# VectorE order in the gate/up stage of a fused attention and MLP kernel: filler sums moved behind quadrant 0, early fill begun three quads sooner

## The chip, the core and the metric

The kernel runs on one core of a Trainium2 chip. The metric is the time of one execution in microseconds of the device ("us"). A profile is one execution recorded by the hardware; its span runs from the core's first instruction to its last and was 1.7 to 1.8 us shorter than the time of the same execution. TensorE is PE, VectorE is DVE, ScalarE is ACT, and SP issues the DMA transfers used here. L851 is line 851 of the kernel.

## The reference, cut to what matters

```python
x = A_x                                    # [1, 2048, 1024] bf16
h = x + attention(layernorm(x), A_wqkv, A_wo)      # linear attention, 32 heads
y = layernorm(h)
gate = y @ W_gate                          # [1024, 3584]
up   = y @ W_up
hh   = where(gate > 0, gate, 0) * up       # Relu(gate) * up
h2   = h + hh @ W_down                     # [3584, 1024]
```

The stage in question is gate, up and their product (gate/up), some 287 to 584 us of the trace; the down projection follows.

## The kernel before

The kernel multiplies by a scheme with seven block products instead of eight (m1 to m7, each 8 matmuls: four contraction steps for gate and four for up). In gate/up a **quad** is the four output quadrants of one block of features. Every group of four quads shares a second-level product of 28 matmuls, p1 to p7, spread over the first quad of the group: that first quad's time is called the product window here. TensorE accumulates in three kinds of PSUM bank, ACT copies snapshots out, and DVE adds a snapshot to a bank (`gu`), after which ACT applies the Relu and DVE multiplies:

```python
# in quad()
def m(n, nm, t=None):                       # 8 matmuls into bank A, D or E
    ...
            nc.tensor.matmul(ps[:, v, :], lhsT=w[v][n - 1][:, kc, :], rhs=left[n - 1][:, kc, :], ...)   # L851
def snap(nm):
    nc.scalar.copy(out=st[nm][:], in_=halves(st["A"]))                                            # L856
def gu(q, nm, base):
    g = st[q] = mwork.tile([P, 2, SW], BF16, tag="gu", name="gu")
    add(out=g[:], in0=halves(st[nm]), in1=st[base][:], op=ALU.add)                                # L860
    nc.scalar.activation(out=g[:, 0, :], in_=g[:, 0, :], func=ACT.Relu)                           # L861
def mul(q):
    add(out=out[q], in0=st[q][:, 0, :], in1=st[q][:, 1, :], op=ALU.mult)                          # L864
def mul2():
    add(out=out[2], in0=halves(st["A"])[:, 1, :], in1=st["rg"][:], op=ALU.mult)                   # L871
    hh_sums_a(hq, s, fc)                                                                          # L700-702
# [... cut ...]
"g0": lambda: gu(0, "A", "r") if first is not None else gu(0, "D", "m1"),
"m6": lambda: m(6, "A"), "m3": lambda: m(3, "E"), "m4": lambda: m(4, "A"), "g3": lambda: gu(3, "E", "u3"),
"g1": lambda: gu(1, "E", "u2"), "x1": lambda: (mul(1), hh_sums_b(hq, s, fc)),   # hh_sums_b: L708
# [... cut ...]
```

Two pairs matter: m6 accumulates into bank A once g0 has read it, and m3 accumulates into bank E (accX or accY by turns) once g3 has read it. Between these reads DVE does small sums that later quads and the down projection need, here called filler. They are the sums of the next quad's weights (L642 to 648), of the second-level operands (L893 to 896, L919), of four rows of hh that an earlier stage spilled to HBM, and of W_down:

```python
def wd_sums(c):
    ...
    def one():
        t = fpool.tile([P, FQ * SW], BF16, tag="wt", name="wt")       # a single buffer
        ...
        tt(out=st["t"][0], in0=b12, in1=b11, op=ALU.subtract)         # L680
    def two(): ...                                                    # L683
    def three(): ...                                                  # L686
    def four():
        tt(...)                                                       # L689
        for k in range(4):
            nc.sync.dma_start(out=t_dram[k][:, 2 * c:2 * c + 2, :], in_=st["t"][k])   # L691
    return load, [one, two, three, four]

def hh_sums_a(hq, s, f):
    ...
    nc.vector.tensor_tensor(out=s1, in0=hq[:, H21, :], in1=hq[:, H22, :], op=ALU.add)   # L700
    nc.vector.tensor_tensor(out=s2, in0=s1, in1=h11, op=ALU.subtract)                   # L701
    nc.vector.tensor_tensor(out=s3, in0=h11, in1=hq[:, H21, :], op=ALU.subtract)        # L702
    nc.sync.dma_start(out=x_dram[s][k][:, H22:S3 + 1, r, :], in_=hq[:, H22:S3 + 1, :])

def early_sums(f):                          # one spilled row: 5 pieces, two of them empty
    ...
    return [load, lambda: None, lambda: None, lambda: hh_sums_a(st[0], 0, f), lambda: hh_sums_b(st[0], 0, f)]
```

The filler of one quad lies in a list `work`, which six slots empty in program order. PE, DVE and ACT run in that order; only the order of DMA issue is left to a scheduler. There are 24 quads: four alone, then five groups of four.

```python
def slot(n):
    for _ in range(-(-len(work) // (SLOTS - n))):       # SLOTS = 6
        work.pop(0)()
# per quad, k counts quads, r counts feature blocks
if grouped:
    want = -(-len(fill) // max(nwin - 2 - k, 1))        # nwin = 24; fill: 55 pieces
    for p in range(want):
        work.insert(min(len(work), 2 * p + 1), fill.pop(0))
elif r in (1, 2):
    for p in range(2 if r == 1 else 1):
        work.append(cross_sums.pop(0))
# product window (first quad of a group); x is the second-level product, prv the quad before
x["p1"](); x["c1"](); prv["g3"](); x["p2"](); x["j00"](); prv["m4"]()
slot(0)
prv["x3"](); prv["m3"](); prv["rg"](); prv["x2"](); x["p6"](); x["c2"](); x["p5"](); prv["g1"]()
slot(1)
prv["x1"](); cur = quad(s, f, w, res[s, fi]); cur["m1"](); x["p7"](); x["c3"]()
slot(2)
cur["g0"](); cur["m5"]()
# [... cut: next weights' loads ...]
x["j11"](); slot(3); cur["m6"](); cur["s2"](); cur["x0"](); x["p4"](); x["c4"]()
slot(4); x["p3"](); x["j01"](); cur["m7"](); cur["s3"](); slot(5)
# [... cut: the other quads ...]
if k == nwin - 3:
    for x in range(2):
        ...
        load_w(0, x)                                    # first W_down tiles, 896 KB each, L977
```

(Statements are joined on lines here to save room.)

## Time and profile before

The median is 738.5 us over 3 runs, 736.57 to 738.87; the profiled run has a span of 734.7 us. By stretch, from the table of windows (busy us of each engine):

| stretch, us | length | PE busy | DVE busy | ACT busy |
|---|---|---|---|---|
| 0 to 287.2 (attention, first MLP rows) | 287.2 | 278.96 | 214.07 | 192.03 |
| 287.2 to 584 (gate/up) | 296.8 | 293.71 | 250.31 | 128.91 |
| 584 to 734 (down projection) | 150.0 | 146.90 | 116.05 | 4.05 |

TensorE is busy nearly throughout, and DVE for 84% of gate/up. A busy share does not tell a lost half microsecond, however, since records of matmuls overlap, and a few are missing. Gaps in this document are therefore taken from starts: 0.2157 us is laid against every matmul, and what the next start has beyond that is a gap (lost records show as whole multiples of 0.2157 behind a group of less than four, and are left out). Before the change gate/up has five, one in each group; the prediction shows their lines. Gaps here are good to about 0.01 us: their sum is 2.56 us in the prediction and 2.55 in the tables.

### The profile page before, as it was taken

Reading aid. Unit: us, or ns where it says so; the run is one execution under the profiler, and the core shown is the slowest. Engines: PE = TensorE matmul, PEld = TensorE weight load, DVE = VectorE, ACT = ScalarE, POOL = GpSimd, SP = SyncE. Lnnn points to the kernel's source line nnn. Section 1 sums busy time; section 2 is a strip of 40 time slices with the busy share of each in tenths; the row PEclk is TensorE's granted clock in tenths of the full one; section 3 lists DMA queues with packets and bytes.
Section 4 is the critical chain, followed back from the end, with each engine's and each line's share of the span. In section 5 each row is a group of like instructions: output and inputs, shape, how many; then the busy total and the mean of one; then the engine's idle time right before and its main releaser. Section 6 shows DMA issues by size and latency. Waiting matters only on the chain.

```text
span 734.7 us, 10578 instructions
## 1 busy us (share of the span) xinstructions
PE 719.6 (98%) x3947; PEld 380.0 (52%) x4000; DVE 580.4 (79%) x1039; ACT 325.0 (44%) x580; POOL 20.8 (3%) x56
## 2 busy tenths in 40 slices
PE   8999999999999999999999999999999999999997
PEld 3444555444444444444444444444444468888567
DVE  6998644677789767789897898989987379996677
ACT  4876553778886655444444444444444220000000
POOL 1000000000000000000000000000000001100210
PEclk9999999999999999999999999999999999999999
DMA  9765002079986524167348558685574499977932
GB/s 316 168 147 158 0 1 93 24 163 228 232 166 159 136 73 137 43 172 212 98 135 258 180 183 249 210 239 197 187 243 134 144 392 337 311 258 276 258 44 58
DMA packets 144708, 128.89 MB, mean 175 GB/s; under 512 B 50960, under 2 KB 127888, under 8 KB 144656
## 3 DMA queue, kind: packets, MB, share of 16 engines
q1 hardware_dynamic: 137584, 123.30, 55.5%
q0 software_dynamic: 5312, 3.15, 3.6%
q10 hardware_dynamic: 1760, 1.77, 0.7%
q8 instruction: 31, 0.51, 0.3%
q14 instruction: 21, 0.17, 0.1%
HBM read 76.81 MB, written 39.85 MB: 159 GB/s over the span
## 4 chain that ended last, share of the span: by engine, by line
PE 67%; DVE 18%; ACT 7%; DMA 5%; issue 2%; SPq 0%; DVEq 0%; ACTq 0%; POOL 0%
PE accA L851 15%; PE accA L1345 8%; PE attn L557 5%; PE accX L851 4%; PE Aq L314 3%; DVE gu L860 3%; PE accA L1171 3%; PE accY L851 3%; PE Aq L738 3%; PE accX L1345 3%; PE Aq L454 3%; PE accY L1345 2%; PE Eq L314 2%; PE accY L1171 2%; PE accX L1171 2%
## 5 line engine op out<-in xcount | busy, mean ns | idle before, releaser
L861 ACT ACTIVATE gu<-gu 128x512 bf16<-128x512 bf16 x72 | 45.5, 632 | 84.0 <-DVE gu L860 84.0
L856 ACT COPY snap<-accA 128x1024 f32<-128x1024 f32 x52 | 52.5, 1012 | 65.2 <-PE accA L851 65.0
L851 PEld LDWEIGHTS <-tg 128*128 128x128 f16 x384 | 37.5, 98 | 47.9 <-issue 3.2
L851 PEld LDWEIGHTS <-tu 128*128 128x128 f16 x384 | 37.6, 98 | 45.3
L557 PE MATMUL attn<-wo_mem,oT 128*128 128x512 bf16 x247 | 57.9, 379 | 1.9 <-DVE o_sb L534 1.2
L851 PE MATMUL accA<-hn,tg 128*128 128x512 f16 (+1 forms) x192 | 49.3, 379 | 0.0
L851 PE MATMUL accA<-hn,tu 128*128 128x512 f16 (+1 forms) x192 | 49.3, 379 | 0.0
L154 ACT COPY u<-Aq 128x512 f32<-128x512 f32 x54 | 31.4, 583 | 36.4 <-PE Aq L314 19.1
L1345 PEld LDWEIGHTS <-x 128*128 128x128 f16 (+1 forms) x448 | 43.8, 98 | 5.5
L557 PEld LDWEIGHTS <-oT 128*128 128x128 bf16 x256 | 24.6, 98 | 31.8 <-issue 3.4
L860 DVE TENSOR_TENSOR gu<-accX,snap 128x1024 bf16<-128x1024 f32 x26 | 31.7, 1221 | 10.6 <-ACT snap L856 8.3
L860 DVE TENSOR_TENSOR gu<-accY,snap 128x1024 bf16<-128x1024 f32 x26 | 31.7, 1220 | 7.5 <-ACT snap L856 7.5
L851 PEld LDWEIGHTS <-wu 128*128 128x128 bf16 x208 | 20.4, 98 | 24.5
L851 PEld LDWEIGHTS <-wg 128*128 128x128 bf16 x208 | 20.4, 98 | 24.5
L314 PEld LDWEIGHTS <-xT 128*128 128x128 bf16 (+1 forms) x192 | 18.6, 98 | 23.5 <-issue 2.1
L534 DVE TENSOR_TENSOR o_sb<-nd,rd 128x384 bf16<-128x384 f32 (+1 forms) x48 | 23.4, 509 | 8.3 <-ACT rd L533 6.1
L1309 POOL DMA_DIRECT2D out_dram<-o x12 | 15.2, 1265 | 506.5 <-DVE o L1305 504.7
L1345 PEld LDWEIGHTS <-xs 128*128 128x128 f16 x280 | 27.4, 98 | 3.2
L560 DVE SCALAR_TENSOR_TENSOR x_res<-attn,x_res 128x512 bf16<-128x512 f32 x32 | 22.0, 687 | 8.5 <-PE attn L557 8.4
L1351 DVE TENSOR_TENSOR snap<-accA,u 128x1024 f32<-128x1024 f32 x16 | 19.5, 1221 | 11.4 <-PE accA L1345 11.3
L864 DVE TENSOR_TENSOR hq<-gu 128x512 bf16<-128x512 bf16 x48 | 20.3, 423 | 10.3 <-ACT gu L861 10.3
L1171 PEld LDWEIGHTS <-x 128*128 128x128 bf16 (+1 forms) x168 | 16.5, 98 | 19.6
(268 smaller groups left out, 1508.9 us busy)
## 6 DMA issues: line engine op xcount, KB each, us to landing
x<-x_dram SPq DMA_DIRECT2D x17, 896.0 KB, 8.5
x_dram<-hq SPq DMA_DIRECT2D x28, 512.0 KB, 3.1
wg<-in_B_W_gate_dram SPq DMA_DIRECT2D x14, 512.0 KB, 4.9
wu<-in_B_W_up_dram SPq DMA_DIRECT2D x14, 512.0 KB, 6.6
x_dram<-hq SPq DMA_DIRECT2D x28, 256.0 KB, 2.4
wraw<-in_B_W_down_dram SPq DMA_DIRECT2D x14, 512.0 KB, 5.1
t_dram<-wt SPq DMA_DIRECT2D x21, 256.0 KB, 2.4
xd<-x_dram SPq DMA_DIRECT2D x6, 896.0 KB, 6.7
```

The lines of the kernel that those rows point to most:

```text
L154: copies[nm, v] = nc.scalar.copy(out=snaps[nm, v], in_=bank[v][:])
L314: nc.tensor.matmul(ps[:], lhsT=left[m - 1][:, kc, r + v * P:r + (v + 1) * P], rhs=right[m - 1][:, kc, :], start=(start and kc == 0), stop= ...
L454: nc.tensor.matmul(ps[:], lhsT=rq[m - 1][:, kc, (c + v) * P:(c + v + 1) * P], rhs=left[m - 1][:, kc, :], start=(start and kc == 0), stop=( ...
L534: nc.vector.tensor_tensor(out=ov[:, c0:c0 + n], in0=ndv[:, :, 0:P].rearrange("p k (h e) -> p k h e", h=HPC), in1=rd[:, 0:n, :].unsqueeze(3 ...
L557: nc.tensor.matmul(ps[:], lhsT=st["oT"][:, c, :], rhs=wo_sb[:, c, j * NW:(j + 1) * NW], start=(c == 0), stop=(c == KC - 1))
L738: nc.tensor.matmul(ps[:], lhsT=w(v, m)[:, kc, :], rhs=left[m - 1][:, kc, :], start=(start and kc == 0), stop=(kc == KH - 1), skip_group_ch ...
L851: nc.tensor.matmul(ps[:, v, :], lhsT=w[v][n - 1][:, kc, :], rhs=left[n - 1][:, kc, :], start=(t is not None and kc == 0), stop=(kc == KH - ...
L856: nc.scalar.copy(out=st[nm][:], in_=halves(st["A"]))
L860: add(out=g[:], in0=halves(st[nm]), in1=st[base][:], op=ALU.add)
L861: nc.scalar.activation(out=g[:, 0, :], in_=g[:, 0, :], func=ACT.Relu)
L1171: nc.tensor.matmul(ps[:, t * NW:(t + 1) * NW], lhsT=x_tile(n, s, kh)[:, f, (t0 + t) * P:(t0 + t + 1) * P], rhs=w_tile(n, kh)[:, f, :], sta ...
L1345: nc.tensor.matmul(pv[:, tt, :], lhsT=left(m)[:, f, tt * P:(tt + 1) * P], rhs=right(m)[:, f, :], start=(t is not None and f == 0 and tt % ...
```

## The change

Intent: take the filler away from the place ahead of g0, where it holds up m6, and put it next to the second-level join behind it; let the first two slots of the product window take less; and begin the fill at the second quad rather than the fifth, so that fewer pieces fall into each later window.

```diff
-    def slot(n):
-        for _ in range(-(-len(work) // (SLOTS - n))):
+    def slot(n, parts=0):
+        for _ in range(-(-len(work) // (parts or SLOTS - n))):
             work.pop(0)()
...
-            if grouped:
+            if r in (1, 2):
+                for p in range(2 if r == 1 else 1):
+                    work.append(cross_sums.pop(0))
+            if k:
                 want = -(-len(fill) // max(nwin - 2 - k, 1))
                 for p in range(want):
                     work.insert(min(len(work), 2 * p + 1), fill.pop(0))
-            elif r in (1, 2):
-                for p in range(2 if r == 1 else 1):
-                    work.append(cross_sums.pop(0))
...
                 prv["m4"]()
-                slot(0)
+                slot(0, 9)
                 prv["x3"]()
...
                 prv["g1"]()
-                slot(1)
+                slot(1, 8)
                 prv["x1"]()
...
                 x["c3"]()
-                slot(2)
                 cur["g0"]()
+                slot(2, 4)
                 cur["m5"]()
```

## The prediction

> **What bounds the kernel now.** I read the page's busy times, the chain, the table of windows over gate/up (287 to 584 us), the waits of that stretch, then the timeline wherever a matmul starts late.
>
> ```profile
> PE 719.6 (98%) x3947; PEld 380.0 (52%) x4000; DVE 580.4 (79%) x1039; ACT 325.0 (44%) x580; POOL 20.8 (3%) x56
> ...
> PE 67%; DVE 18%; ACT 7%; DMA 5%; issue 2%; SPq 0%; DVEq 0%; ACTq 0%; POOL 0%
> ```
> TensorE is the bound; DVE's 18% of the chain suggests more than there is, since much of it ran beside matmuls.
>
> ```profile
> 344.00:392.00 48.00, 47.43 (x216) 21.52 (x220) 42.37 (x86) 21.61 (x28) 0.00 (x0) 1.00 0.49 158
> ```
> Columns: window, length, then busy us and count of PE, weight loads, DVE, ACT. One group of four quads is four times six steps of 8 matmuls plus one second-level product of 28, so 220. Eight matmuls take 1.73 us in the chain, 0.2157 each: 220 make 47.45 us. Groups follow each other every 47.8 us, so a group loses about 0.4 us, although DVE is 88% busy.
>
> ```profile
> PE accA L851 <- DVE gu L860: 1.8, 4, 0.8
> ```
> This is the only wait of TensorE in the whole stretch.
>
> I then laid 0.2157 us per matmul against all starts. Where 0.21 us is missing a group shows x3 for x4: a lost record. Five real gaps remain, each at m6, which accumulates into bank A, behind quadrant 0's `gu<-accA`:
>
> ```profile
> 344.31 1.02 PE L851 MATMUL accA<-hs,tg 128*128 128x512 f16 x4 [0.83 <-DVE gu L860]
> 392.12 1.02 PE L851 MATMUL accA<-hs,tg 128*128 128x512 f16 x4 [0.17 <-DVE gu L860]
> 439.98 1.02 PE L851 MATMUL accA<-hs,tg 128*128 128x512 f16 x4 [0.22 <-DVE gu L860]
> 487.60 1.02 PE L851 MATMUL accA<-hs,tg 128*128 128x512 f16 x4
> 535.80 1.02 PE L851 MATMUL accA<-hs,tg 128*128 128x512 f16 x4 [0.56 <-DVE gu L860]
> ```
> By start-to-start they are 0.99, 0.33, 0.38, 0.14 and 0.72 us: 2.56 us, or 0.35% of 738.5. That is all this change can win in gate/up.
>
> DVE ahead of the first gap:
>
> ```profile
> 340.77 0.43 DVE L864 TENSOR_TENSOR hq<-gu 128x512 bf16<-128x512 bf16 x1 [0.43 <-ACT gu L861]
> 341.23 0.42 DVE L708 TENSOR_TENSOR hq<-hq 128x512 f16<-128x512 bf16 x1
> 341.57 0.42 DVE L647 TENSOR_TENSOR tu<-wu 128x512 f16<-128x512 bf16 x1
> 341.91 0.42 DVE L700 TENSOR_TENSOR hq<-hq 128x512 f16<-128x512 bf16 x1
> 342.36 0.43 DVE L701 TENSOR_TENSOR hq<-hq,x 128x512 f16<-128x512 f16 x1
> 342.70 0.42 DVE L702 TENSOR_TENSOR hq<-x,hq 128x512 f16<-128x512 bf16 x1
> 343.04 1.22 DVE L860 TENSOR_TENSOR gu<-accA,snap 128x1024 bf16<-128x1024 f32 x1
> ```
> Here 647 and the spilled-row sums 700 to 702 are filler; g0 (L860) ran from 343.04 to 344.26 because of them, and m6 would have started at 343.32.
>
> **What the Trainium skill says.** "TensorE: Matmul & The Clock Gate", section "Wait — 56ns, not 53.3ns?": warm 512-column matmuls start 215.7 ns apart; the trace agrees (1.73 us for 8; each record shows 379 ns). "VectorE: DVE Perf Modes", "The perf-mode tier table": tensor_tensor runs 2x on bf16 in SBUF and 1x with a PSUM operand; here 424 ns for 512 16-bit elements against 1219 ns for 1024 out of PSUM. "PSUM — Partial Sum Buffer", "PSUM bank collisions raise a hardware error": guard PSUM by bank, so a matmul may not write a bank that VectorE reads; every gap above is such a wait, ending 0.05 us after the reader (344.26, 344.31). "Perfetto Trace Analysis", "Per-instruction lifecycle": DVE is strict FIFO; so the order of the program decides, as those seven rows in program order show.
>
> **The change, part by part.** Nothing is added or removed: the listing of instruction order has 955 DVE instructions before and after, PE and ACT unchanged. Only DVE's order and DMA issue change.
>
> Durations used are start-to-start: 0.34 us for a 512-element sum (0.45 where it takes the result just made), 0.61 for a 1024-element one, 1.14 for L860, 1.13 for 700 to 702, 0.35 for the 708 behind them.
>
> (a) Behind quadrant 0. In each of the five product windows the slot before g0 moves behind it. In groups 2 to 5 all that remains from g3 to g0 is one weight sum and at most one filler, and that filler sits in the 0.42 us that DVE waits for ACT's Relu anyway. For group 2, 700 to 702 (1.13) and 708 (0.35) go: g0 moves from 390.85 to 389.38, ending at 390.6, while m6 is due at 391.79. Gap gone. Group 3 loses a 1024-element sum (0.61) against a gap of 0.38; groups 4 and 5 lose two (1.22) against 0.14 and 0.72. I count all four as gone: 0.33 + 0.38 + 0.14 + 0.72 = 1.57 us won. The second-level join now comes after two fillers, but had 1.5 us of slack (ended 393.20, its bank wanted at 394.71) and stays inside it.
>
> (b) Fill three quads sooner. Each window from the second quad on now takes three fill pieces, so the second takes loads only; the third takes 700 to 702 and 708 of row 0 (1.13 + 0.35); the fourth 700 to 702 of row 1 (1.13). That is 2.6 us more DVE work before the first product window, and DVE has little idle there:
>
> ```profile
> 320.86 0.43 DVE L864 TENSOR_TENSOR hq<-gu 128x512 bf16<-128x512 bf16 x1 [0.43 <-ACT gu L861]
> ...
> 324.18 0.43 DVE L864 TENSOR_TENSOR hq<-gu 128x512 bf16<-128x512 bf16 x1 [0.70 <-ACT gu L861]
> ...
> 326.50 0.43 DVE L864 TENSOR_TENSOR x<-gu 128x512 bf16<-128x512 bf16 x1 [0.76 <-ACT gu L861]
> ```
> The first 0.43 is used up. The other two are the time of a Relu between `gu` and its product and stay, as nothing is placed in them: the fourth quad's first two fill pieces are empty and the third lands after the product. Step by step: third quad's g0 at 314.37 instead of 313.58, g1 at 319.5 for 318.88; fourth quad's g3 at 323.25 for 322.27, g0 at 325.6 for 324.53, x0 at 327.55 for 326.50, then the fill, x2 at 329.0 for 326.99. From there DVE ran without a break until 340.35, so the 2.0 us carry over to g3 of the first product window, at 335.7 for 333.66:
>
> ```profile
> 333.66 1.22 DVE L860 TENSOR_TENSOR gu<-accY,snap 128x1024 bf16<-128x1024 f32 x1
> ...
> 335.55 1.03 PE L851 MATMUL accY<-hs,wg 128*128 128x512 f16 x4
> ```
> m3 adds to the bank g3 reads. It had 335.55 - 334.88 = 0.67 us of slack; 2.04 of delay make it wait about 1.4 us. A new stall. After it g0 (no filler ahead, 1.47 us less) comes at 343.6 to 344.8, and m6 is due at 343.32 + 1.4 = 344.7: a stall of about 0.1 instead of 0.99. So group 1 costs 1.4 + 0.1 - 0.99 = +0.5 us.
>
> (c) Later windows carry three or two fill pieces instead of three or four; TensorE waits nowhere there, so that is worth nothing. DMA bytes are the same and the fill ends in the same window.
>
> Sum: -1.57 + 0.5 = -1.1 us: 738.5 - 1.1 = 737.4. One of the three runs before was 736.57 and the profiled one 736.51, so the median leans high; I choose 737.2.
>
> **Rivals.** 1. The early fill costs nothing, and all 2.56 us are won: about 735.9. For it: 1.9 us of DVE idle in the third and fourth quads; the windows here show DVE only 88% busy. Against: two of the three idles are Relu latency. 2. The early fill costs more than reckoned: the later Relu holds the snapshot behind it on ACT (ended 333.31, m4 due at 333.82; my shift makes it 333.8), or the loads of spilled rows are late. With another 1 to 2 us: 738.5 to 739.5. Against the loads: the x rows issue at 289, 24 us ahead of their first use. 3. The wait behind g0 moves on: m7 behind the next snapshot, or the join, takes the gap, so that groups 2 to 5 win only half: 738.0. Against: that snapshot ended 347.24 with m7 at 347.76, and both move with m6. 4. The weight loads, queued behind the early stores, come late. Against: they move by 1 to 2 us and are read over 10 us later.
>
> **Range and chances.** The sums span 735.9 to 739.5, and single runs of one kernel spread 2.3 us; 735.2 to 739.0 should hold it 8 times in 10. Faster by 2% would need 14.8 us, six times all the gaps: 0.01. Slower by 2% would need some twenty new stalls of 0.7 us: 0.01. Within 2%: 0.98.
>
> **What would show it right or wrong.** (a) m6 of groups 2 to 5 has no gap, and group-to-group distance is 47.5 instead of 47.8 us. (b) A wait of m3 (accY) on `gu` L860 near 335.5 of about 1.4 us, and 0.1 to 0.2 at m6 near 345; if m3 has none, rival 1 holds. If m4 or p5 near 334 to 340 waits, rival 2. If the span outside 287 to 584 us changes by more than 0.5 us, the cause lies where I did not look, in DMA order.

## The result, and the profile after

The changed kernel took 735.42 us in the median of 6 runs (734.98 to 737.78), the kernel before 738.18 us in 6 runs of the same rounds (736.57 to 739.43). A ratio in this document is the mean time of one kernel's runs over that of the other's of the same rounds, so not quite the ratio of the medians: here 0.9972, with a 95% interval of 0.9952 to 0.9992. That is faster by 0.3%. Executions over 1.5% slower than the fastest of the same kernel are left out of the means.

The page of the changed kernel, its busy times and its chain:

```profile
PE 720.9 (98%) x4000; PEld 379.7 (52%) x4000; DVE 580.5 (79%) x1039; ACT 323.9 (44%) x580; POOL 20.7 (3%) x56
...
PE 80%; DVE 9%; ACT 5%; DMA 4%; issue 1%; SPq 0%; DVEq 0%; POOL 0%; ACTq 0%
```

The work is the same: 1039 DVE instructions and 580.5 us of it. DVE's share of the chain has fallen from 18% to 9%; that is what a path that leaves DVE looks like, but it is not the gain, since the DVE stretches of the chain lay beside matmuls. The chain reads as a route, the gaps as a cost. The waits of TensorE in gate/up, changed kernel:

```profile
PE accY L851 <- DVE gu L860: 1.1, 1, 1.1
```

One wait is left, on another bank. The timeline of TensorE (start, length, both in us; a bracket gives the idle time before and its releaser):

```profile
336.72 1.02 PE L851 MATMUL accY<-hs,wg 128*128 128x512 f16 x4 [1.05 <-DVE gu L860]
...
344.61 1.02 PE L851 MATMUL accA<-hs,tg 128*128 128x512 f16 x4
...
392.09 1.03 PE L851 MATMUL accA<-hs,tg 128*128 128x512 f16 x4
```

By starts the first gap is 1.22 us (m3) and the second 0.13 us (m6 of group 1). In groups 2 to 5 there is none: m6 starts at 392.09, 439.58, 487.06 and 534.54 us, so the groups follow each other every 47.48 us where they took 47.6 to 48.2 before, and the 220 matmuls of a group alone make 47.45. The table of windows, in the row that the prediction shows for the kernel before:

```profile
344.00:392.00 48.00, 48.00 (x224) 21.71 (x222) 43.52 (x87) 22.00 (x30) 0.00 (x0) 1.00 0.64 202
```

By busy time TensorE has no idle time in it now (which, as said above, does not rule out the 0.13 us at 344.61), and DVE is still at 43.5 of 48 us: the group was never short of DVE time as a whole, only of the right order. g0 of group 2 in the kernel before:

```profile
390.85 1.22 DVE L860 TENSOR_TENSOR gu<-accA,snap 128x1024 bf16<-128x1024 f32 x1
```

and DVE on the way, changed kernel:

```profile
327.31 0.43 DVE L864 TENSOR_TENSOR x<-gu 128x512 bf16<-128x512 bf16 x1 [0.76 <-ACT gu L861]
327.66 0.42 DVE L700 TENSOR_TENSOR hq<-hq 128x512 f16<-128x512 bf16 x1
...
328.79 0.68 DVE L871 TENSOR_TENSOR hq<-accA,rg 128x512 bf16<-128x512 f32 x1
...
335.45 1.22 DVE L860 TENSOR_TENSOR gu<-accY,snap 128x1024 bf16<-128x1024 f32 x1
...
343.34 1.22 DVE L860 TENSOR_TENSOR gu<-accA,snap 128x1024 bf16<-128x1024 f32 x1
...
389.16 0.42 DVE L864 TENSOR_TENSOR hq<-gu 128x512 bf16<-128x512 bf16 x1 [0.76 <-ACT gu L861]
389.62 0.42 DVE L708 TENSOR_TENSOR hq<-hq 128x512 f16<-128x512 bf16 x1
389.96 1.22 DVE L860 TENSOR_TENSOR gu<-accA,snap 128x1024 bf16<-128x1024 f32 x1
```

Read it in three places. At 389.96 g0 of group 2 follows the quad's own 708 sum at once, with no sum of a spilled row between (0.89 us earlier than the 390.85 of before). At 327.66 to 328.79 the spilled-row sums of the early fill stand between the product x and L871. And 0.76 us of idle in front of 327.31 were not used by them. What they took went on to g3 at 335.45, which before ran at 333.66; m3, behind it, is the new wait.

All gaps of gate/up in every kernel, by starts, and the time from the first gate/up matmul to the start of the last group of matmuls of the program:

| kernel | gaps, us | sum | interval | interval less gaps |
|---|---|---|---|---|
| before | m6: 0.99, 0.33, 0.38, 0.14, 0.72 | 2.55 | 442.12 | 439.57 |
| changed | m3 1.22, m6 0.13 (group 1) | 1.34 | 440.90 | 439.56 |
| changed, again | m3 1.23, m6 0.14 | 1.36 | 440.91 | 439.55 |
| slots alone (second build) | m3 in the second quad of group 5, 0.52 | 0.52 | 440.08 | 439.56 |
| early fill alone | m3 1.21, m6 0.80 (group 1), 0.70 (group 3) | 2.70 | 442.26 | 439.56 |
| early fill placed in the Relu waits | none | 0 | 439.56 | 439.56 |
| the same, again | none | 0 | 439.56 | 439.56 |
| slot behind g0 alone | m6 0.36, 0.10; m3 in the second quad of group 5, 2.38 | 2.83 | 442.40 | 439.57 |
| the same, again | m6 0.36, 0.10; the same m3 1.92 | 2.37 | 441.93 | 439.56 |
| the same, load held | m6 0.36, 0.09 | 0.44 | 440.01 | 439.57 |
| slots alone, load held | none | 0 | 439.56 | 439.56 |
| changed, longer filler | p2 0.38, m4 0.76, m3 1.47, m6 0.14 | 2.74 | 442.28 | 439.54 |

The last column is the check of the account: in twelve traces of nine kernels everything outside these gaps takes 439.54 to 439.57 us. So the whole effect of the change on the trace is 2.55 - 1.34 = 1.21 us, and the spans differ by 734.7 - 733.5 = 1.2. The kernel before was traced once. The stages ahead of gate/up end between 286.70 and 288.35 us from run to run, with the same program; that scatter is larger than the effect, and is why spans alone cannot carry the argument.

### The profile page after: what moved, and what is told of

Same layout as the page of the kernel before. It is cut to its first block, busy times and chain, and to the rows that moved or that the text cites. A ratio compares the mean times of both kernels' runs of the same rounds, so it can differ in the third digit from the quotient of the medians.

```text
span 733.5 us, 10630 instructions
## 1 busy us (share of the span) xinstructions
PE 720.9 (98%) x4000; PEld 379.7 (52%) x4000; DVE 580.5 (79%) x1039; ACT 323.9 (44%) x580; POOL 20.7 (3%) x56
## 4 chain that ended last, share of the span: by engine, by line
PE 80%; DVE 9%; ACT 5%; DMA 4%; issue 1%; SPq 0%; DVEq 0%; POOL 0%; ACTq 0%
PE accA L851 21%; PE accA L1345 8%; PE accX L851 6%; PE accY L851 5%; PE attn L557 5%; PE Aq L314 3%; PE Aq L738 3%; PE accA L1171 3%; PE accX L1345 3%; PE Aq L454 3%; PE accY L1345 3%; PE accA L939 2%; PE Eq L314 2%; PE accX L1171 2%; PE accY L1171 2%; PE Eq L738 2%
## 5 line engine op out<-in xcount | busy, mean ns | idle before, releaser
L864 DVE TENSOR_TENSOR hq<-gu 128x512 bf16<-128x512 bf16 x48 | 20.2, 421 | 10.0 <-ACT gu L861 9.8
```

## The experiments

Theory, as in the prediction: (T1) moving the filler behind g0 removes the gaps of groups 2 to 5, and (T2) the early fill costs a new wait at m3 because it lands on DVE's path to g3. Rivals: the early fill costs nothing and only the new order matters; the waits come from loads or stores of spilled rows that are late; the two parts only help together. All results were correct.

### 1. The slots without the early fill

The order in the product window as changed, the fill from the fifth quad on as before.

```diff
-            if r in (1, 2):
-                for p in range(2 if r == 1 else 1):
-                    work.append(cross_sums.pop(0))
-            if k:
+            if grouped:
...
+            elif r in (1, 2):
+                for p in range(2 if r == 1 else 1):
+                    work.append(cross_sums.pop(0))
```

> Slots of the product windows as changed, fill begun where it was before. Theory A (only DVE work between the reader of a bank and the instructions ahead of it counts; the early fill is pure cost): quadrant 0 moves forward by 1.81 us in group 1, 1.11 in group 2 and 0.6 to 1.2 in groups 3 to 5, so all five gaps at m6 close, m3 never waits, the gaps in gate/up sum to 0 (before 2.55, changed kernel 1.34 us) and the profiled span is 2.5 us under before and 1.3 under the changed kernel. Rival B (the early fill takes load off the groups and is needed for the gain): at least half of the gaps of groups 2 to 5 stay, 0.8 us or more.

Measured: 734.38, 734.43, 734.44 and 734.72 us, ratio 0.9962 (0.9947 to 0.9977), and one run of 1969.8 us, which the profile fell into. That trace says nothing of waits of 1 us; it is looked at again at the end. So the slots alone are at least as good as the whole change, by the time; where their gaps lie had to be seen in a second run (experiment 6).

### 2. The early fill without the slots

```diff
-                slot(0, 9)
+                slot(0)
...
-                slot(1, 8)
+                slot(1)
...
+                slot(2)
                 cur["g0"]()
-                slot(2, 4)
```

> Fill begun three quads sooner, slots as before. Theory A: m3 of the first product waits 1.2 us as in the changed kernel; at m6 the gaps are about 0.8, 0, 1.0, 0 and 0 us for groups 1 to 5 (the pieces that happen to stand ahead of quadrant 0 decide, 0.61 us more than before in group 3, 0.9 us less in 2, 4 and 5); sum 3.0 us, so 0.5 us slower than before. Rival B: the lighter groups alone close most gaps and the sum is under 2.0 us, faster than before.

Measured: 736.81 us (736.16 to 737.3), ratio 0.9994 (0.998 to 1.0008). The timeline of TensorE in this kernel:

```profile
336.25 1.02 PE L851 MATMUL accY<-hs,wg 128*128 128x512 f16 x4 [1.05 <-DVE gu L860]
...
344.82 1.02 PE L851 MATMUL accA<-hs,tg 128*128 128x512 f16 x4 [0.64 <-DVE gu L860]
...
440.48 1.02 PE L851 MATMUL accA<-hs,tg 128*128 128x512 f16 x4 [0.53 <-DVE gu L860]
```

The wait at m3 is here in full, 1.21 us by starts, without any change of the slots: it comes from the early fill. The filler ahead of g0 is back too, and m6 waits 0.80 us in group 1 and 0.70 in group 3. Groups 2, 4 and 5 lose their gaps through the other distribution of pieces alone. The sum, 2.70 us, is 0.15 more than before the change: alone, the early fill gains nothing. (Expected were 1.0 us in group 3 and 3.0 in all, so group 3 was put too high.)

### 3. The early fill placed in the Relu waits

The third rival was the tempting one: DVE idles 0.70 and 0.76 us in the fourth quad, so sums could be free there. The pieces of a spilled row are put in such an order that the first sum (L700) lands in the first of these waits and the other two in the second. The sums are the same, but the edit does one thing more: those of row 0 now run one quad sooner.

```diff
-        return [load, lambda: None, lambda: None, lambda: hh_sums_a(st[0], 0, f), lambda: hh_sums_b(st[0], 0, f)]
+        def first():
+            nc.vector.tensor_tensor(out=st[0][:, S1, :].bitcast(FP16), in0=st[0][:, H21, :], in1=st[0][:, H22, :], op=ALU.add)
+        return [load, first, lambda: hh_sums_a(st[0], 0, f, False), lambda: hh_sums_b(st[0], 0, f), lambda: None]
```

(`hh_sums_a(..., False)` leaves out the first sum.)

> The changed kernel, with the pieces of the spilled-row sums in another order and their first sum split off, so that in the fourth quad they fall into the two stretches in which DVE waits for a Relu (0.70 and 0.76 us), and those of row 0 one quad sooner. The same work, the same loads, still early. Theory A: g3 of the first product begins near 334.3 instead of 335.45, m3 waits 0 to 0.1 instead of 1.22 us, no gap at m6; sum 0 to 0.1, the span about 1.2 us under the changed kernel. Rival C (the early pieces wait for their loads or hold up the DMA queue, not DVE's order): the wait of m3 stays above 0.8 us.

Measured: 733.97 us (733.72 to 735.83, 6 runs), ratio 0.9959 (0.9944 to 0.9975). DVE in the fourth quad, with lines 4 lower in the file (L868 is the product L864, L864 is `gu`, 729, 702 and 703 are the sums):

```profile
324.57 0.41 DVE L729 TENSOR_TENSOR hq<-hq 128x512 f16<-128x512 bf16 x1
325.35 0.42 DVE L868 TENSOR_TENSOR hq<-gu 128x512 bf16<-128x512 bf16 x1 [0.36 <-ACT gu L865]
...
326.83 0.41 DVE L702 TENSOR_TENSOR hq<-hq,x 128x512 f16<-128x512 f16 x1
...
327.67 0.42 DVE L868 TENSOR_TENSOR x<-gu 128x512 bf16<-128x512 bf16 x1
...
335.01 1.22 DVE L864 TENSOR_TENSOR gu<-accY,snap 128x1024 bf16<-128x1024 f32 x1
```

The idle of 0.70 us is now 0.36 and that of 0.76 is gone. Gate/up began 0.75 us later in this run than before (287.95 against 287.20), so g3 at 335.01 is 334.26 on that clock: 0.6 us later than before, within the 0.67 us of slack that m3 had. TensorE waits nowhere in gate/up. With the same early fill and the same bytes, the wait at m3 is gone, so neither the loads nor the amount of filler made it, but the place. Counted from the start of gate/up (287.95 here, 287.16 in the changed kernel), L871 of the fourth quad (328.34 here, 328.79 there) comes 1.24 us earlier. Of this 0.43 us is there already at the third quad's g0 (314.56 here, 314.20 there), which is row 0's move, and 0.8 us comes from the two Relu waits. No run shows either of the two alone.

### 4. The changed kernel again, in the same rounds

> The changed kernel once more on the chip of these runs, to compare with in the same rounds. Theory A: gaps of 1.2 us at m3 and 0.1 at the first m6 again, ratio to before 0.998 to 0.999, since 1.2 of 735 us is 0.16%. If the ratio is again 0.997 with the same gaps, something outside gate/up that the two profiles do not show gives about 1 us.

Measured: 735.47 us (734.61 to 736.08), ratio 0.9975 (0.996 to 0.9989) where 0.998 to 0.999 was expected; the gaps are 1.23 and 0.14 us, within 0.01 of the first trace. The four versions of experiments 1 to 4 shared one chip and one series of runs with the kernel before, so their means can be laid beside their gaps:

| kernel | mean, us | less the changed kernel's | by the gaps |
|---|---|---|---|
| fill in the Relu waits | 734.35 | -1.07 | -1.36 |
| slots alone | 734.49 | -0.93 | -0.84 |
| changed | 735.42 | 0 | 0 |
| early fill alone | 736.84 | +1.42 | +1.34 |
| before | 737.43 | +2.01 | +1.19 |

Among the four versions the gaps tell the time to 0.3 us or better. The kernel before is slower than its gaps say, by 0.8 us here; more on that below. (For the slots the gaps are those of experiment 6.)

### 5. The moved slot alone

To part the moved slot from the smaller first slots, only slot 2 goes behind g0, with its old share; the fill starts as before.

```diff
 (against the kernel before)
                 x["c3"]()
-                slot(2)
                 cur["g0"]()
+                slot(2)
```

> Only one edit: the third slot of the product windows behind quadrant 0, with six equal slots and the fill where it was. Theory A, by what still stands ahead of quadrant 0: group 1 loses 1.47 us and has no gap, group 2 loses 0.35 and has none or 0.05, group 3 has nothing in that slot and keeps 0.38, group 4 loses 0.61 and has none, group 5 loses 0.61 and keeps 0.1 of 0.72. Sum about 0.5 instead of 2.55 us, span 2.0 us under before. Rival: the fewer pieces in the first two slots do the work, and over 1.3 us of gaps stay.

Measured, one look: 736.48 us, span 734.7, while the kernel before took 738.55 us in the run beside it. At m6 only 0.36 (group 3) and 0.10 us (group 5) are left of 2.55: the moved slot is worth 2.1 us of the gaps at m6, and the smaller first slots the rest. But a gap of 2.38 us has come up at 544.39 us, at m3 in the second quad of group 5. The lines of DVE, TensorE and of SP's DMA issues in this kernel:

```profile
541.05 0.69 DVE L680 TENSOR_TENSOR wt<-wraw 128x1024 f16<-128x1024 bf16 x1 [5.32 <-DMA xd<-x_dram]
...
544.39 1.02 PE L851 MATMUL accY<-hs,wg 128*128 128x512 f16 x4 [2.22 <-DVE gu L860]
...
532.68 0.42 SPq L977 DMA_DIRECT2D wd<-in_B_W_down_dram  x1
533.96 0.33 SPq L691 DMA_DIRECT2D t_dram<-wt  x1
```

and the issues of the kernel before:

```profile
534.64 0.33 SPq L691 DMA_DIRECT2D t_dram<-wt  x1
535.07 0.40 SPq L977 DMA_DIRECT2D wd<-in_B_W_down_dram  x1
```

L680 is the first of four sums into the single buffer `wt`, and has to wait until the stores of the sums before it have left that buffer. Before, the store was issued ahead of the 896 KB load of W_down; here it is issued 1.28 us behind it. Stores from `wt` took 2.3 us in the median from issue to landing; this one took 6.9 and so landed at 540.8, some 0.2 us before L680 began. The Trainium skill, "DMA: Bandwidth & Descriptors", section "Queues, rings and completion order", says that an SDMA engine consumes the descriptors of a ring in order, which fits a store that has to pass behind such a load. The profile names another transfer as the releaser (`xd<-x_dram`, issued right behind the store). By the same trace that one, issued at 534.38, took 10.0 us and landed only at 544.4, 3.3 us after L680 had begun, so it cannot have released it. That the load delayed the store still had to be tested. DVE, being in program order, stood still for 5.32 us, and everything behind it was late.

### 6. Slots alone once more, the moved slot with the load held, and the moved slot once more

The first is the kernel of experiment 1. In the second the two W_down loads are issued one quad later and tied to a product of that quad, which keeps them behind the store; all else is as in experiment 5.

```diff
-            if k == nwin - 3:
+            if k == nwin - 2:
                 for x in range(2):
                     ...
+                    hold(wtiles[x][0:1, 0, 0:1], x1[s][f // FQ][0:1, f % FQ, 0:1])
                     load_w(0, x)
```

> The slots-only kernel again, since its profile fell in a run of 1970 us[...]. Theory A: no gap at m6 in any group and none at m3 of group 1. Added after the move-only run (theory D: a filler can hold DVE by a DMA: the first sum of a W_down piece overwrites the one buffer whose store queued behind a 0.9 MB load): here too that store stands behind the load in the queue, the sum two fillers after it, so m3 of the second quad of group 5 may wait 1.5 to 2.5 us. If it does, the span is 0.2 to 1 us under before; if not, 2.5 us.

> Move-only, with the two first W_down loads of the last stage held until the products of quad 22, so that the stores of the W_down sums go ahead of them in the queue. Nothing else differs in the order of PE, DVE or ACT. Theory D: the first sum of the next piece no longer waits 5.3 us for the store of the one before, the 2.38 us gap of m3 in group 5 is gone, the gaps sum to 0.46 (0.36 and 0.10 at m6) and the span falls by about 2.4 us. If the gap stays over 1.5 us, the cause is not the load ahead of the store. The later load itself is needed some 25 us after its new start and should cost nothing.

> Move-only unchanged, to see whether the wait of 5.3 us before the first W_down sum and the 2.38 us gap of m3 in group 5 come back. Theory D: the same order of the queue, so a gap of 1.5 to 2.5 us again; if it was chance, none.

Measured: slots alone 735.47 us (734.67 to 736.43), ratio 0.9979 (0.9961 to 0.9997); one look each at the moved slot with the load held, 734.15 us, and without, 736.33 us. The kernel before had a median of 736.93 us in these rounds. With the load held, DVE and the issues:

```profile
536.33 0.69 DVE L680 TENSOR_TENSOR wt<-wraw 128x1024 f16<-128x1024 bf16 x1 [0.55 <-DVE x L864]
...
534.01 0.33 SPq L691 DMA_DIRECT2D t_dram<-wt  x1
...
544.56 0.38 SPq L977 DMA_DIRECT2D wd<-in_B_W_down_dram  x1
```

The wait of 5.32 us (4.85 in the second trace of the same kernel) is now 0.55, the store lands in 2.1 us, the gap at m3 of group 5 is gone, and the two small ones at m6 stay at 0.36 and 0.09. The load issued ahead of the store was the cause. Whether it acts by its place in the queue or by being under way at all, this run cannot tell, since the load is away altogether. The kernel before speaks for the place: there the store went 0.43 us ahead of the same load and landed in 2.7 us.

Slots alone, the kernel with the best time in the first rounds, has the same fault in small: L680 waits 3.63 us, the releaser named there is `t_dram<-wt` itself (5.2 us to landing, issued 1.1 us behind the load), and m3 of group 5 starts 0.52 us late. A gap of 1.5 to 2.5 us had been expected there, so the kind was right and the size too large by a factor of three or more. In the changed kernel this wait is absent. Its early fill shifts the W_down sums against the windows, and the first sum into `wt` starts at 530.8 us, ahead of the second W_down load at 532.95. So the early fill, which costs 1.2 us at m3 of group 1, saves about 0.5 us at the end of gate/up.

### 7. A longer filler, to measure the wait one for one

If the filler on DVE's way to g3 makes the wait, more of it must make more. The second of the three sums of row 1 is issued four times instead of once (the same values, so the result stays correct).

```diff
-        nc.vector.tensor_tensor(out=s2, in0=s1, in1=h11, op=ALU.subtract)
+        for _ in range(1 + more):           # more = 3 for row 1 of the early fill, else 0
+            nc.vector.tensor_tensor(out=s2, in0=s1, in1=h11, op=ALU.subtract)
```

> The changed kernel with one 512-element sum of spilled row 1, in the fourth quad, done three times more (same operands, same result): 3 x 0.34 = 1.0 us more DVE work ahead of g3 of the first product. Theory A: one for one, m3 waits 2.2 to 2.3 us instead of 1.22, m6 keeps its 0.1, the span is 1.0 us longer than the changed kernel's. Rival C (a late load sets the wait): the extra sums are hidden in part and m3 waits less than 1.8 us.

Measured, one look: 736.61 us, span 734.8. The lines of DVE and TensorE (all lines here one lower in the file):

```profile
328.08 1.81 DVE L702 TENSOR_TENSOR hq<-hq,x 128x512 f16<-128x512 f16 x4
...
334.88 1.02 PE L852 MATMUL accA<-hn,tg 128*128 128x512 bf16 x4 [0.60 <-ACT snap L857]
...
338.07 1.02 PE L852 MATMUL accY<-hs,wg 128*128 128x512 f16 x4 [1.30 <-DVE gu L861]
```

The next sum starts at 329.80, so the four take 1.72 us where one takes 0.34: 1.38 more. The gaps grow from 1.36 us in the changed kernel's second trace to 2.74, by 1.38. One for one, then, in the sum (the dose was 1.38 us and not the 1.0 expected); but not at one place. TensorE now waits first at p2 (0.38 us, for the bank that g1 reads), then at m4 (0.76 us, for ACT's snapshot, which the later Relu delays), and m3's wait grows only to 1.47, as it is late already. By the letter of what was expected, an m3 below 1.8 us spoke for rival C, a late load; the sum speaks against it, since nothing of the dose was hidden. The wait at m4 is rival 2 of the prediction, the Relu holding back the snapshot, which comes up at this delay (no smaller dose was tried).

### 8. The two best versions: slots with the load held, and the fill in the Relu waits

Slots alone with the load held as in experiment 6, beside the kernel of experiment 3. The third is a second build of the first, for a trace.

> Slots only (fill where it was before) with the W_down loads held as in the run before. Theory A with D: no gap at m6, none at m3, the sum in gate/up 0 (slots only had 0.52, all at m3 of group 5 behind the store of a W_down sum), so from the first to the last matmul group of gate/up to the end 439.6 us and a ratio to before of 0.9965, the same as the kernel with the pieces in the Relu's idle time. If a gap of 0.3 us or more stays in group 5, the load ahead of the store was not what held it.

> The kernel with the early pieces in the Relu's idle time again, beside the one above: no gaps, ratio to before 0.9965; the two within 0.1% of each other, since neither has a gap left.

> The slots-only kernel with the loads held, once more for its profile, since the one before fell in a run of 2713 us. Theory A with D: no gap of TensorE in gate/up, none at m3 of group 5; from the first matmul of gate/up to the last group of matmuls 439.6 us, and a span of 732 to 733. A gap of 0.3 us or more in group 5 would mean that the load ahead of the store was not the cause in the slots-only kernel.

Measured: slots with the load held 734.52 us, or 734.0 without one run of 2713.31 (733.32 to 735.12), ratio 0.9954 (0.994 to 0.9969); the fill in the Relu waits 734.0 us (733.41 to 735.11), ratio 0.9953 (0.9939 to 0.9966), both about 0.1% under the 0.9965 expected. The means of their runs stand at 1.0002 to one another. The profile of the first fell into the slow run, so one more look was taken: 735.12 us in its single run (span 733.4, as gate/up began only at 288.35), and no gap at all in gate/up. Both have an interval of 439.56 us: they have reached what the matmuls of this program take back to back, and reordering DVE can win nothing more there. Of the two, the fill in the Relu waits is the one to keep: it needs no later load, and its mean was 0.9985 of the changed kernel's in the same rounds (734.35 over 735.42).

Not tested: a second buffer for `wt`, the plain remedy for the wait at L680.

### The very long runs

Experiments 1 and 8 each had one execution of 1970 or 2713 us, and the kernel before had one of 2713.19 us too, so this is not a matter of the version. The same window of two of them, slots alone first and slots with the load held second (the first is in gate/up then, the second still ahead of it):

```profile
800.00:1000.00 200.00, 200.00 (x337) 59.16 (x336) 66.25 (x131) 32.64 (x43) 0.00 (x0) 1.00 0.19 57
```

```profile
800.00:1000.00 200.00, 200.00 (x263) 56.82 (x262) 44.88 (x109) 36.68 (x82) 0.00 (x0) 1.00 0.14 36
```

337 and 263 matmuls in 200 us are 0.59 and 0.76 us on average. One by one, matmuls of 512 columns start 0.62 or 0.49 us apart in the first trace and 0.84 or 0.68 in the second, against 0.2157 in a normal run. The clock of 1.00 says nothing here: neither trace holds a clock record, where each of the normal ones has two, and without records 1.00 is printed. A whole run has 597.0 us of DVE work in the first case, hardly more than the 580.5 of a normal one, and `gu` took 1.22 us as always; TensorE's weight loads did take longer (690.0 for 379.7 us). So TensorE was slow and VectorE was not. Why is open.

## Why the prediction was right or wrong

**Step (a), the gaps of groups 2 to 5: right.** All four are gone, 1.57 us as said. g0 of group 2 was put at 389.38 and ran at 389.96. The way from g3 to g0 did shrink, by 1.48 us where 1.47 was reckoned (before from 381.81 to 390.85, after from 382.40 to 389.96, 9.04 and 7.56 us), but g3 itself came 0.59 us later: DVE had idled 0.80 us in front of it before, and the filler of the changed order lies there now. It did no harm, as g0 ended at 391.18 and m6 was due at 392.09. The distance of groups is 47.48 us, as foretold with 47.5. What did it is shown by experiment 5 with its load held: the moved slot takes 2.55 us down to 0.44, and the smaller first slots (experiment 8) the rest.

**Step (b), the early fill: right in kind and close in size.** The wait is at m3, on accY, as foretold, with 1.22 us for about 1.4, and m6 has 0.13 for about 0.1. The reckoning ran g3 to 335.7, and it came at 335.45; it was already 0.17 us ahead at g0 of the third quad (314.20 for 314.37) and 0.24 at the fourth quad's product (327.31 for 327.55). Group 1 thus costs 1.22 + 0.13 - 0.99 = +0.36 us, where the prediction had +0.5. Experiments 2, 3 and 7 show the cause: the wait is there with the early fill alone, gone when the same sums lie elsewhere (in the Relu waits, and row 0's a quad sooner), and the gaps grow one for one with a longer sum.

**Step (c), "worth nothing": not quite.** The trace of the changed kernel agrees, but only because its parts do not add. Slots alone leave 0.52 us (2.03 won), the early fill alone 2.70 (0.15 lost); the sum of both would be 1.88 won, and together they win 1.21. The gaps of groups 2, 4 and 5 (1.19 us) are removed by each part alone and so counted twice in 1.88; against that stand 0.52 us of the store's wait in group 5, which the prediction did not see and which only the new slots without the early fill have, and smaller shifts at m6 of groups 1 and 3, which cancel.

**The sum.** Foretold -1.1 us, in the traces -1.21. The median of the kernel before was 738.5 and then 738.18 us, that of the changed one 735.42, so the timed difference is larger, -2.1 us by the means with an interval of 0.6 to 3.5. So no wait was badly sized, but the timed number, 735.42 for 737.2, is 1.8 us off, and it lies only 0.2 us inside the lower end of the range. The forecast took 1.1 us from a base of 738.3, close to the 738.18 that the kernel before then took. Laid from the profiled run, whose gaps were counted, it would have been 736.51 - 1.1 = 735.4; that this is the number measured is partly luck, since single runs of the kernel before went from 736.57 to 739.43. What the forecast missed is that part of the timed difference which no gap accounts for. The account by gaps lies within every interval measured but at the edge of some: before exceeds the account by 0.9, 0.8 and 1.0 us in three series (this one, that of experiment 4, that of experiment 8) and falls short of it by 0.5 in the fourth (experiment 6). Whether an untraced run of the kernel before loses something that its single trace does not have was not settled, and the 0.3% of the timed result is only in part, 1.2 of 2.1 us, explained.

**The rivals.** Rival 1 (early fill free) was false for the changed kernel, and experiment 3 shows what would have made it true. Rival 2 (later Relu and snapshot) has no part in the change, and appears at 1.38 us of further delay; its other half, late loads, is refuted by experiment 3. Rival 3 (the wait moves on to m7 or the join) did not come: no gap at all behind m6. Rival 4 (weight loads) did not show in the changed kernel. A DMA-order effect did show in two of the part versions (slots alone, moved slot alone), but of the W_down load against a store, not of the weights. The prediction's 955 DVE instructions come from a listing; the traces count 1039 before and after, which bears out the same point.

## What to carry to other kernels

When an engine runs in program order and has little idle time, ask of each filler instruction which read of a shared bank stands behind it: the same sums cost 1.2 us where they first stood, and nothing a little earlier, in the waits for a Relu and one quad sooner. Judge changes of half a microsecond by gaps from start to start over the whole stage, checked by the remainder that must stay constant, and not by spans or medians, which scatter more than that. And a part that looks better alone may have moved a transfer in the queue: look at the order of issue wherever a single buffer is stored and reused.

## What the Trainium skill lacked or had wrong

- "TensorE: Matmul & The Clock Gate", section "What's actually happening", lists two states, a cold and a warm clock; further down, in "Seeing it yourself", it mentions a clock stuck at a quarter for 50 us and more. Executions of 1970 and 2713 us had matmuls of 512 columns 0.62 or 0.49 and 0.84 or 0.68 us apart from beginning to end, against 0.2157 in a normal run. The page's cold clock starts such matmuls 426.7 ns apart, and a quarter clock would make it about 0.85 us, an estimate from that figure, which is near the 0.84 and not near the other three; no cause is known from these runs.
- "VectorE: DVE Perf Modes" gives the tiers, which agree, but not what a sum costs that uses the result just made: 0.45 us from start to start against 0.34 for an independent one (L700 to L701 and L701 to L702), and 0.46 for a sum repeated into the same tile (three repeats took 1.38 us).
- "DMA: Bandwidth & Descriptors", section "Queues, rings and completion order", has the order of a ring but no figure for what a small store loses behind a large load: in experiment 5, 256 KB stores took 2.0 us at the least and 2.3 in the median, and 6.9 us where one was issued 1.28 us behind an 896 KB load.
- No page says that the releaser that a profile names for a wait need not be the one at fault: in experiment 5 a wait of 5.32 us was put down to a load that landed 3.3 us after the wait had ended, and delaying another transfer, issued ahead of it, cut the wait to 0.55 us.
